# A retimed order of attention, and the combine weights' splits between the experts' relus, in a fused attention and soft-MoE kernel

## The chip, the cores and the metric

The kernel runs as one program on one core of a Trainium2 chip. Its time is what the device takes for one execution, in microseconds. The core's engines are TensorE (PE; its weight loads are shown apart as PEld), VectorE (DVE), ScalarE (ACT), GpSimd (POOL) and SyncE (SP), which here issues nearly all transfers. Each engine works through its own list of instructions in order and waits at an instruction until what it needs is there.

## What is computed

First comes attention with a memory, for 8 batches and 8 heads of 576 positions and 64 columns; its output is laid out as 4608 rows of 512 and goes through a soft mixture of 8 experts with 4 slots each.

```python
scores = np.where(causal, -1e9, scale * q @ k.T)
local  = softmax(scores) @ v
q_p    = where(q > 0, q, exp(q) - 1) + 1
mem    = (q_p @ M_prev) / (q_p . z_prev + 1e-6)
x      = g * mem + (1 - g) * local            # g = sigmoid(beta) per head
logits = x @ phi                              # 4608 x 32
slot_in = softmax(logits, over rows).T @ x    # 32 x 512
slot_out[e] = relu(slot_in[e] @ w1[e]) @ w2[e]
out    = softmax(logits, over slots) @ slot_out
```

All inputs are float32. The expert weights alone are 32 MB (64 tiles of 512 KB).

## The kernel before

**The attention** is done in 32 steps n = 0 to 31, one for each batch and pair of heads (`@n` in the tables). The order in which all its small operations are written is a table, SEQ, with 2546 entries, each the name of an operation, its step and, for the ones that take a PSUM bank, the bank's number behind a colon. A second table, EV, says for each copy and some arithmetic which engine does it (`a` ScalarE, `v` VectorE, `p` GpSimd). A loop calls `op_<name>` entry by entry, and `pin()` then fixes every engine's instructions in just this order. WORD says into which freed tile the last weight tiles are loaded.

The operations that matter below:

- `loadq`, `loadk`, `loadv`, `loadm`: a step's inputs, each one transfer on SP; `w@x`: one weight tile of 512 KB on SP.
- `qhi`, `qlo`, `kn`, `kl` (L359, L403, L409): q and k split into a rounded part and a rest for the score products `s.*` (L414, L433, L441); `max.*` (L470), `exp.*` (L478), transposes `t.*` (L567), their copies `te.*` (L354, L357).
- `qmin`, `qexp`, `qphi` (L510 on ScalarE or L512 on GpSimd, L515, L519): the feature map, in the tile `qp`, of which there is one for even and one for odd steps.
- `norm`, `neps`, `nmk`, `nred` (L525 to L542): the memory's normaliser. `nrw` (L547) writes it to a scratch in DRAM, `rd`; `nrr` (L553) reads it back, spread over the partitions, as `rb`; `qn` (L557) multiplies it into `qp`; `mema` uses that.
- `rec` (L483, L484), `rt`, `rte`: the softmax's reciprocal; `rrw` (L498 to L500) writes it to DRAM as `rs`, `rrr` (L504) reads it back into a part of the tile `rm`; `mo` (L631) and `xe.0` (L638, L639) multiply the local output with it, `xe.1` (L642) adds the memory's. `rb` and this part of `rm` exist once, so each read waits for the last use of the step before.
- `x*` and `y*`: the slots' running softmax and sums, once for every finished block of 512 rows, with the last block in `y*`.

**The tail** is ordinary code behind the table (L1015 to L1051): `f1(eg, f)` multiplies the slots with w1 (16 matmuls in float32, shown as 32 by the profile) and applies the relu on ScalarE (L940); `f1t` transposes the result; `f2(dh, eg, f)` multiplies with w2 and sums over all eg, f into one PSUM bank per output half dh. `c1`, `c2` do the last two blocks' softmax over slots and its transposes; `c3(i, j)` splits the transposed combine weights `cT` into a rounded part, twice, by ScalarE, and a rest, by VectorE (L989), for tile j of `cst4` (i = 0, 32 x 1024) or of `cst8` (i = 1, 32 x 128). `g1`, `g2` scale and split the slots' output; `comb(dh, t4)` makes 512 rows of an output half in two PSUM banks (4 matmuls), which ScalarE and VectorE copy out, one each, and SP stores them (512 KB). 20 weight tiles are loaded during the tail, into the tiles that the first `f1` have read. PSUM there: two banks for `f1` and `f2`, two for `f1t`, `c1`, `c2`, `g2`, four for `comb`.

Of the kernel before, what the change touches and what calls it, by code (L numbers as in the profile page):

```python
# [51 lines left out]
max.q2h0@1 t.3@0:1 rte@0 exp.a@1 qphi@1 t.4@0:0 rrw@0 exp.b@1 s.z@1:0 max.q3h0@1 te.4@0 te.3@0 te.1@0 loadk@3 s.q1@1
exp.q2h0@1 norm@1:3 max.q3h1@1 av.0@0:0 kn@2 max.q1h0@1 exp.q3h0@1 max.z@1 s.b@2:1 qn@0 av.1@0 neps@1 exp.z@1 nmk@1
rrr@0 s.a@2 av.2@0 max.q1h1@1 exp.q1h0@1 qhi@2 nred@1 mema@0:21 exp.q1h1@1 qlo@2 max.a@2 nrw@1 kl@2 exp.q3h1@1 av.6@0
memb@0 loadm@2 av.3@0 qmin@2 exp.q2h1@1 s.zb@2 loadq@3 s.q2@2 loadv@1 rec@1 s.q1@2:0 max.b@2 max.zb@2 t.0@1:3 exp.b@2
xe.0@0 s.z@2 te.0@1 nrr@1 mo@0 rt@1:1 t.5@1:3 xe.1@0 rte@1 qexp@2 t.4@1:0 rrw@1 max.q1h0@2 te.5@1 t.1@1:1 max.q1h1@2
t.3@1:2 max.q2h1@2 te.1@1 t.2@1:3 max.q2h0@2 loadk@4 exp.a@2 x3.0@0:1 te.3@1 max.z@2 te.4@1 s.q3@2:1 qphi@2 exp.q1h0@2
s.zb@3:0 qhi@3 max.q3h0@2 av.0@1:2 te.2@1 loadq@4 kn@3 x3e.0@0 qn@1 rrr@1 s.b@3 exp.q1h1@2 norm@2:0 kl@3 max.q3h1@2
av.3@1 exp.q2h1@2 mema@1:13 qlo@3 exp.q3h1@2 max.zb@3 neps@2 av.6@1 nmk@2 qmin@3 loadm@3 exp.q2h0@2 s.q3@3:1 nred@2
exp.z@2 s.q2@3 max.q3h1@3 nrw@2 exp.q3h0@2 av.1@1 max.q2h0@3 max.q3h0@3 exp.q3h1@3 memb@1 av.2@1 xe.0@1 qexp@3 loadv@2  # L60
s.q1@3:1 rec@2 exp.q2h0@3 qphi@3 t.1@2:0 rt@2:3 nrr@2 s.z@3 max.b@3 rte@2 mo@1 exp.q3h0@3 s.a@3 kn@4 norm@3:3
max.q1h0@3 te.1@2 max.q2h1@3 rrw@2 t.3@2:2 qhi@4 neps@3 t.0@2:0 xe.1@1 te.3@2 kl@4 t.4@2:3 te.0@2 exp.q2h1@3 loadq@5
t.2@2:1 loadk@5 qlo@4 te.4@2 t.5@2:2 nmk@3 t.0@3:0 max.a@3 te.2@2 max.q1h1@3 t.2@3:3 nred@3 exp.a@3 qn@2 x3.1@0:1
te.5@2 nrw@3 x3e.1@0 s.q2@4:0 rrr@2 exp.q1h0@3 av.0@2:2 av.2@2 te.0@3 s.zb@4 s.b@4 te.2@3 max.z@3 av.6@2 s.a@4
mema@2:01 exp.b@3 nrr@3 max.zb@4 exp.z@3 av.1@2 max.q2h1@4 qmin@4 loadm@4 max.q2h0@4 memb@2 exp.q1h1@3 av.3@2 max.b@4
exp.q2h1@4 max.a@4 loadv@3 s.q3@4:1 xe.0@2 loadk@6 rec@3 exp.a@4 s.q1@4:0 mo@2 rt@3:3 s.z@4 rte@3 xe.1@2 qexp@4 rrw@3
t.1@3:1 qn@3 exp.b@4 max.z@4 t.4@3:2 te.1@3 t.3@3:3 max.q1h0@4 te.4@3 qphi@4 t.5@3:0 qhi@5 te.3@3 mema@3:21 max.q3h1@4
qlo@5 te.5@3 max.q1h1@4 kn@5 norm@4:3 qmin@5 s.zb@5:0 exp.q1h0@4 av.0@3:0 neps@4 rrr@3 nmk@4 nred@4 s.a@5 s.b@5 av.3@3
kl@5 nrw@4 qexp@5 memb@3 av.2@3 max.zb@5 loadm@5 exp.z@4 x1.0@0:3 qphi@5 av.1@3 exp.q1h1@4 max.q3h0@4 exp.q2h0@4
av.6@3 s.q2@5 exp.q3h1@4 xe.0@3 s.q3@5:1 nrr@4 exp.q3h0@4 mo@3 t.3@4:1 xe.1@3 t.1@4:0 loadv@4 te.3@4 max.q3h1@5 x1.1@0  # L70
loadq@6 te.1@4 norm@5:2 rec@4 loadk@7 x1l@0 t.4@4:1 neps@5 max.a@5 max.q3h0@5 rt@4:0 t.0@4:3 rte@4 te.4@4 x1m@0
t.5@4:2 rrw@4 s.z@5:1 te.0@4 x1e@0 qn@4 t.2@4:0 max.b@5 exp.q3h1@5 w@1 te.5@4 x2@0:1 te.2@4 s.q1@5 max.q2h1@5
exp.q3h0@5 av.0@4:3 max.q1h1@5 max.q2h0@5 qhi@6 exp.b@5 av.1@4 max.q1h0@5 kn@6 max.z@5 exp.q1h0@5 rrr@4 memb@4:2
s.zb@6:0 qlo@6 exp.q2h0@5 s.a@6 kl@6 mema@4:0 exp.q2h1@5 x2m@0 loadq@7 nmk@5 s.b@6 exp.q1h1@5 qmin@6 max.b@6 s.q3@6:1
exp.a@5 nred@5 exp.z@5 max.a@6 av.6@4 nrw@5 av.2@4 max.q3h0@6 av.3@4 max.q3h1@6 exp.q3h0@6 loadv@5 s.q2@6 mo@4 qexp@6
s.q1@6:1 rec@5 x2a@0 s.z@6 exp.a@6 xe.1@4 t.2@5:3 qhi@7 xe.0@4 nrr@5 t.3@5:1 max.q1h0@6 te.2@5 kn@7 rt@5:0 t.0@5:2
te.3@5 rte@5 qlo@7 max.q2h0@6 t.5@5:3 loadm@6 te.0@5 max.q2h1@6 t.4@5:0 rrw@5 te.5@5 kl@7 t.1@5:1 qphi@6 x2e@0
x3.3@0:2 te.4@5 max.q1h1@6 x3.2@0:3 loadq@8 te.1@5 max.zb@6 max.z@6 loadk@8 s.q3@7:0 exp.q2h1@6 qn@5 s.b@7:1
max.q3h1@7 x4.0@0:0 s.a@7 max.q3h0@7 s.zb@7 x3e.3@0 av.0@5:1 rrr@5 x3e.2@0 exp.q3h1@6 norm@6:2 max.a@7 av.1@5
exp.q2h0@6 max.zb@7 x4a.0@0 w@2 neps@6 exp.b@6 memb@5:3 x2s@0 av.6@5 mema@5:0 exp.z@6 exp.q1h1@6 nmk@6 av.2@5 nred@6  # L80
qmin@7 exp.q1h0@6 av.3@5 exp.q3h1@7 x4.1@0:2 nrw@6 xe.0@5 loadm@7 s.q2@7 rec@6 loadk@9 qexp@7 s.q1@7:0 x4a.1@0 loadv@6
mo@5 t.2@6:3 rt@6:2 s.z@7 xe.1@5 rte@6 rrw@6 te.2@6 t.0@6:1 kn@8 t.3@6:2 max.b@7 te.0@6 qhi@8 t.5@6:0 nrr@6 te.3@6
t.4@6:3 qlo@8 qphi@7 te.5@6 t.1@6:1 te.4@6 max.q1h0@7 x3.0@1:2 kl@8 max.z@7 te.1@6 x5@0:0 av.0@6:3 exp.a@7 max.q2h1@7
rrr@6 max.q1h1@7 av.6@6 norm@7:1 max.q2h0@7 av.3@6 neps@7 s.q3@8:0 exp.q1h0@7 loadq@9 nmk@7 exp.q3h0@7 nred@7 av.2@6
qn@6 x5e@0 nrw@7 s.zb@8:1 exp.z@7 s.a@8 av.1@6 w@3 max.q3h0@8 exp.b@7 mema@6:01 max.q3h1@8 exp.q1h1@7 exp.q2h0@7 mo@6
s.b@8 qmin@8 loadm@8 memb@6 exp.q2h1@7 xe.1@6 s.q1@8:0 loadv@7 s.q2@8 exp.q3h0@8 nrr@7 rec@7 xe.0@6 s.z@8 qexp@8
max.zb@8 max.a@8 max.q2h0@8 t.4@7:3 kn@9 x3e.0@1 qhi@9 rt@7:0 t.1@7:1 te.4@7 kl@9 rte@7 t.3@7:2 max.b@8 rrw@7 te.1@7
max.q2h1@8 x3.1@1:0 max.z@8 t.2@7:3 x3e.1@1 qlo@9 t.0@7:1 max.q1h0@8 loadk@10 t.5@7:0 qphi@8 te.0@7 qn@7 s.q3@9:1
te.3@7 max.q1h1@8 te.5@7 exp.z@8 s.q2@9:0 exp.q2h1@8 norm@8:1 rrr@7 s.zb@9 mema@7:02 neps@8 exp.q3h1@8 max.zb@9 nmk@8
max.q3h1@9 exp.b@8 av.0@7:1 w@4 te.2@7 qmin@9 loadq@10 nred@8 s.b@9 exp.q2h0@8 memb@7 av.1@7 max.q3h0@9 nrw@8 qexp@9  # L90
loadm@9 max.b@9 s.a@9 av.3@7 exp.q1h0@8 qphi@9 av.6@7 av.2@7 exp.a@8 exp.q1h1@8 mo@7 loadv@8 s.q1@9:1 exp.q3h1@9
# [193 lines left out]
def tile_attn_soft_moe(ctx, tc, q, k, v, M, beta, phi, w1, w2, cst, out):  # L285
# [718 lines left out]
    def comb(dh, t4):  # L1004
# [8 lines left out]
        nc.sync.dma_start(out=out[512 * t4:512 * t4 + 512, 256 * dh:256 * dh + 256].rearrange("(u a) d -> a u d", a=128), in_=o)  # L1013
# [104 lines left out]
```

## Time and profile before

| | us |
|---|---|
| median of 3 runs | 483.08 (481.46 to 484.53) |
| the profiled execution | 482.45 |
| its span, first to last instruction | 480.7 |
| PE busy | 431.5 (90%) |
| DVE busy | 378.3 (79%) |
| ACT busy | 341.2 (71%) |
| POOL busy | 168.8 (35%) |

Times in the profile count from the first instruction of the span. A row of busy groups gives the line, engine and operation, `out<-in` with shapes, the count, then busy us, mean ns of one, and the idle time just ahead of them with what ended it. A row of waits reads: engine, line, `<-` what ended the wait, then us in total, times, longest. A piece of the chain that ended last is: start, length, engine or DMA, and what. The chain follows back, from the end, what released each step. DMA share is the mean busy share of the core's 16 DMA engines. PE busy counts the modelled length of each matmul.

### The profile page before, as it was taken

Reading aid. Unit: us, or ns where it says so; the run is one execution under the profiler, and the core shown is the slowest. Engines: PE = TensorE matmul, PEld = TensorE weight load, DVE = VectorE, ACT = ScalarE, POOL = GpSimd, SP = SyncE. Lnnn points to the kernel's source line nnn. Section 1 sums busy time; section 2 is a strip of 40 time slices with the busy share of each in tenths; the row PEclk is TensorE's granted clock in tenths of the full one; section 3 lists DMA queues with packets and bytes.
Section 4 is the critical chain, followed back from the end, with each engine's and each line's share of the span. In section 5 each row is a group of like instructions: output and inputs, shape, how many; then the busy total and the mean of one; then the engine's idle time right before and its main releaser. Section 6 shows DMA issues by size and latency. Waiting matters only on the chain.

```text
span 480.7 us, 15438 instructions
## 1 busy us (share of the span) xinstructions
PE 431.5 (90%) x5762; PEld 288.1 (60%) x5762; DVE 378.3 (79%) x1289; ACT 341.2 (71%) x1001; POOL 168.8 (35%) x155
## 2 busy tenths in 40 slices
...
GB/s 259 152 204 163 114 243 192 216 195 146 157 190 238 209 222 166 203 155 181 192 218 199 179 234 243 202 261 169 222 202 145 157 275 285 244 412 410 154 342 312
DMA packets 65658, 104.09 MB, mean 217 GB/s; under 512 B 10608, under 2 KB 40880, under 8 KB 65584
## 3 DMA queue, kind: packets, MB, share of 16 engines
...
q10 hardware_dynamic: 288, 0.09, 0.1%
...
## 4 chain that ended last, share of the span: by engine, by line
PE 32%; DMA 27%; DVE 21%; ACT 5%; POOL 5%; issue 4%; SPq 4%; DVEq 0%; POOLq 0%; ACTq 0%
DMA rb<-rd 10%; DMA rm<-rs 9%; PE psT L414 9%; DVE q L470 4%; PE psS L441 4%; PE psT L567 4%; PE pf L937 3%; DVE zq L470 3%; DMA rd<-rq 3%; DVE qp L519 2%; DVE at L357 2%; PE pc L1011 2%; ACT w L354 2%; POOL qp L557 2%; PE pf L954 2%
## 5 line engine op out<-in xcount | busy, mean ns | idle before, releaser
L414 PE MATMUL psT<-at,mv 128*32 128x64 f32 (+4 forms) x1536 | 103.4, 389 | 2.3 <-DMA mv<-in_v_dram 2.1
L354 ACT COPY at<-psT 128x256 f32<-128x256 f32 (+1 forms) x209 | 87.3, 481 | 23.9 <-PE psT L567 21.4
L478 ACT ACTIVATE q<-q,nm 128x384 f32<-128x384 f32 (+2 forms) x160 | 97.7, 614 | 8.4 <-DVE nm L470 5.7
L470 DVE CUSTOM_DVE_ANT_0 q<-psS,mv 128x512 f32<-128x512 f32 (+1 forms) x128 | 76.6, 612 | 5.0 <-PE psS L441 2.6
L441 PE MATMUL psS<-K,X 64*128 64x512 f32 (+2 forms) x576 | 72.3, 364 | 5.0 <-DVE nm L470 2.6
L567 PE MATMUL psT<-cs,q 128*128 128x128 f32 x480 | 70.0, 275 | 1.2 <-ACT q L478 0.6
L478 ACT ACTIVATE zq<-zq,nm 128x256 f32<-128x256 f32 (+2 forms) x128 | 68.0, 536 | 3.0 <-DVE nm L470 2.9
L441 PEld LDWEIGHTS psS<-K,X 64*128 64x128 f32 x576 | 45.2, 184 | 27.5 <-issue 9.5
L414 PEld LDWEIGHTS psT<-at,mv 128*32 128x32 f32 x1536 | 40.4, 110 | 32.6 <-issue 20.6
L567 PEld LDWEIGHTS psT<-cs,q 128*128 128x128 f32 x480 | 55.6, 141 | 4.0 <-issue 1.0
L557 POOL TENSOR_TENSOR qp<-qp,rb 128x576 f32<-128x576 f32 x23 | 33.5, 1458 | 53.1 <-DMA rb<-rd 39.0
L567 PE MATMUL psT<-cs,zq 128*128 128x128 f32 x288 | 46.8, 279 | 3.7 <-DVE xt L631 3.3
L512 POOL TENSOR_SCALAR qp<-qq 128x576 f32<-128x576 f32 x19 | 31.8, 1672 | 42.6 <-PE psT L414 41.2
L414 PE MATMUL psT<-qp,q 128*32 128x64 f32 (+1 forms) x512 | 37.3, 408 | 5.0 <-POOL qp L557 2.7
L567 PEld LDWEIGHTS psT<-cs,zq 128*128 128x128 f32 x288 | 34.1, 143 | 6.0 <-DVE xt L631 3.7
L409 POOL TENSOR_TENSOR K<-k,K 128x512 fp32r<-128x512 f32 x25 | 35.6, 1424 | 1.3 <-DVE K L357 0.4
L631 DVE TENSOR_TENSOR xt<-psT,rm 128x448 f32<-128x448 f32 (+7 forms) x60 | 23.6, 432 | 12.9 <-DMA rm<-rs 8.8
L414 PEld LDWEIGHTS psT<-qp,q 128*32 128x32 f32 x512 | 15.0, 109 | 31.0 <-issue 19.5
L357 DVE COPY at<-psT 128x512 f32<-128x512 f32 (+1 forms) x52 | 29.4, 585 | 4.6 <-PE psT L567 1.9
L359 POOL TENSOR_SCALAR K<-k 128x512 fp32r<-128x512 f32 x22 | 14.9, 675 | 50.6 <-PE psS L433 29.2
L519 DVE SCALAR_TENSOR_TENSOR qp<-qq,qp 128x576 f32<-128x576 f32 x32 | 31.1, 973 | 0.3 <-ACT qp L515 0.2
L478 ACT ACTIVATION_READ_ACCUMULATOR q<-q,nm 128x1 f32 x160 | 31.3, 196 | 0.0
...
## 6 DMA issues: line engine op xcount, KB each, us to landing
...
```

What stands on the lines that cost most here:

```text
L354: nc.scalar.copy(o, i)
L357: nc.vector.tensor_copy(out=o, in_=i)
L409: ALU_ENG[ev("kl", n)].tensor_tensor(out=K2[:, 1, :], in0=st[n]["k"][:, 0:512], in1=K2[:, 0, :].bitcast(F32), op=ALU.subtract)
L414: nc.tensor.matmul(o[32 * g:32 * g + 32], w[:, 32 * g:32 * g + 32], x(g), start=start, stop=stop)
L441: nc.tensor.matmul(ps[:, c0:c0 + N], X[ROW[h], x, 128 * i - 128:128 * i], K2[ROW[h], y, 0:N], start=(x, y) == (0, 0), stop=(x, y) == (0, 1))
L470: nc.vector.tensor_tensor_reduce(out=sm, in0=src, in1=msk, op0=ALU.add, op1=ALU.min, scale=-0.125, scalar=m0, accum_out=acc_o)
L478: nc.scalar.activation(sm, sm, AF.Exp, scale=-1.0, bias=s["nm"][:, J:J + 1], accum_out=s["sum"][:, J:J + 1])
L512: ALU_ENG[ev("qmin", n)].tensor_scalar(out=st[n]["qp"], in0=st[n]["q"], scalar1=0.0, scalar2=None, op0=ALU.min)
L519: ALU_ENG[ev("qphi", n)].scalar_tensor_tensor(out=t, in0=st[n]["q"], scalar=0.0, in1=t, op0=ALU.max, op1=ALU.add)
L557: ALU_ENG[ev("qn", n)].tensor_tensor(out=s["qp"], in0=s["qp"], in1=s["rb"], op=ALU.mult)
L567: nc.tensor.transpose(out=ps[:, 128 * x:128 * x + 128], in_=src[:, k0:k0 + 128], identity=ident)
L631: nc.vector.tensor_tensor(out=o, in0=st[n]["oa"][:, c0:c1], in1=rr[:, 64 + c0:64 + c1], op=ALU.mult)
```

## The change

SEQ has the same 2546 operations in another order, with other PSUM banks; EV gives some of them to another engine; WORD has other numbers. The tables' first lines show their kind:

```diff
-gate@0 loadq@1 loadm@0 loadk@1 w@0 qmin@0 qhi@0 qlo@0 qexp@0 kn@0 s.zb@0:0 s.a@0 s.b@0 kl@0 qmin@1 qphi@0 loadk@2
+gate@0 loadm@0 loadq@1 w@0 loadk@1 loadm@1 loadv@0 qmin@0 qhi@0 qlo@0 qexp@0 kn@0 s.a@0:0 s.zb@0 s.b@0 kl@0 qphi@0
```

In EV, `qmin` goes from 13 on ScalarE and 19 on GpSimd to 22 and 10; `qlo` from 14 on VectorE and 18 on GpSimd to 7 and 25; `kn` from 7 on ScalarE, 3 on VectorE and 22 on GpSimd to 2, 2 and 28; `kl` from 7 on VectorE to 6, `qhi` from 5 to 4, `nmk` from 16 to 19, `neps` from 21 to 20 (the rest on GpSimd, for `neps` on ScalarE); the copies `te` stay at 152 and then 151 on ScalarE of 192. 

In the table the distances between a transfer's issue and what uses it change. Mean number of entries over the 32 steps, before and now: `nrw` to `nrr` 23.5 and 31.2, `nrr` to `qn` 32.2 and 36.3, so `nred` to `qn` 60.8 and 74.4; `rrw` to `rrr` 26.9 and 33.1, `rrr` to the first of `mo` and `xe.0` 29.7 and 30.5 (the smallest 15 and 21), so `rec` to that first use 74.6 and 80.5.

What this does on an engine, VectorE in step 19, from the reciprocal of its normaliser on, before:

```order
L542 RECIPROCAL rq<-rq 128x9
L483 SCALAR_TENSOR_TENSOR r<-sum,rm 128x9
L484 RECIPROCAL r<-r 128x9
L638 TENSOR_TENSOR xt_3327<-psT_4124,rm 128x64
L639 TENSOR_TENSOR xt_3327<-xt_3327,psT_4124 128x64
L631 TENSOR_TENSOR xt_3327<-psT_4083,rm 128x192
L631 TENSOR_TENSOR xt_4154<-psT_4083,rm 128x320
L470 ISA q_4174,nm<-psS_4068,mv 128x384
L470 ISA nm 128x1
L642 TENSOR_TENSOR xt_3327<-xt_3327,psT_4129 128x192
```

and now:

```order
L543 RECIPROCAL rq<-rq 128x9
L471 ISA q_4079,nm<-psS_4056,mv 128x512
L471 ISA nm 128x1
L358 COPY at<-psT_4033 128x2x256
L471 ISA q_4112,nm<-psS_4068,mv 128x384
L471 ISA nm 128x1
L471 ISA q_4112,nm<-psS_4068,mv 128x384
L471 ISA nm 128x1
L708 TENSOR_REDUCE s_4141<-rm 128x4
L709 TENSOR_SCALAR s_4141<-s_4141 128x4
L710 RECIPROCAL s_4141<-s_4141 128x4
L711 TENSOR_TENSOR rm<-rm,s_4141 128x128
```

Before, the previous step's row `rm` is used three rows behind the reciprocal; now the first use (`xt<-psT,rm`) stands sixteen rows behind it, and the multiply with `rb` that follows, L557 (now L558), 44 rows behind it where it was 35.

SP in steps 30 and 31 (`rd`, `rb`: normaliser; `rs`, `rm`: softmax row; `in_w`: weights; L389 loads v), before:

```order
L500 DMA rs<-rts 2x1x64
L754 DMA qq<-in_w_dram 128x1024
L754 DMA K_6511<-in_w_dram 128x1024
L754 DMA q_6520<-in_w_dram 128x1024
L504 DMA rm<-rs 64x576 x2
L547 DMA rd<-rq 128x9
L757 DMA zq<-in_w_dram 128x1024
L757 DMA X<-in_w_dram 128x1024
L498 DMA rs<-rts 2x3x128
L499 DMA rs<-rts 2x2x64
L500 DMA rs<-rts 2x1x64
L389 DMA mv<-in_v_dram 128x768
```

and now:

```order
L755 DMA K_6482<-in_w_dram 128x1024
L554 DMA rb<-rd 64x4x144 x2
L505 DMA rm<-rs 64x576 x2
L548 DMA rd<-rq 128x9
L755 DMA X<-in_w_dram 128x1024
L755 DMA qq<-in_w_dram 128x1024
L499 DMA rs<-rts 2x3x128
L500 DMA rs<-rts 2x2x64
L501 DMA rs<-rts 2x1x64
L390 DMA mv<-in_v_dram 128x768
L554 DMA rb<-rd 64x4x144 x2
L758 DMA zq<-in_w_dram 128x1024
```

The two halves of the read of step 30's row (`rm<-rs ... x2`) stand behind three weight loads before, and behind one weight load and the read of `rb` of the same step now; the loads of X and qq follow it.

The tail is written in another order:

```diff
             (act, dve)[half](o[:, 2 * half:2 * half + 2, :], ps)
         nc.sync.dma_start(out=out[512 * t4:512 * t4 + 512, 256 * dh:256 * dh + 256].rearrange("(u a) d -> a u d", a=128), in_=o)
 
+    c1(7)
+    c1(8)
     f1(0, 0)
+    c2(7)
+    c2(8)
     f1(0, 1)
     f1t(0, 0)
-    c1(7)
-    c1(8)
+    c3(0, 0)
+    c3(0, 1)
     f1(1, 0)
     f1t(0, 1)
-    c2(7)
-    c2(8)
+    c3(0, 2)
+    c3(0, 3)
     f1(1, 1)
     f1t(1, 0)
-    c3(0, 0)
     f2(0, 0, 0)
     f1t(1, 1)
     for x, (pool, name) in enumerate(reload):
         wload(nw + x, pool, name)
-    for j in range(1, 4):
-        c3(0, j)
     for j in range(4):
         c3(1, j)
     f2(0, 0, 1)
     f2(0, 1, 0)
     f2(0, 1, 1)
     g1(0)
-    f2(1, 0, 0, (0,))
+    f2(1, 0, 0, (0, 1))
     g2(0)
-    f2(1, 0, 0, (1, 2, 3))
+
+    parts = [(0, 0, (2, 3)), (0, 1, (0, 1)), (0, 1, (2, 3)), (1, 0, (0, 1)), (1, 0, (2, 3)), (1, 1, (0, 1)), (1, 1, (2, 3))]
     for t4 in range(NQ):
         comb(0, t4)
-        if t4 == 4:
-            f2(1, 0, 1)
-    f2(1, 1, 0)
-    f2(1, 1, 1)
-    g1(1)
-    g2(1)
+        if t4 < 7:
+            f2(1, *parts[t4])
+        if t4 == 6:
+            g1(1)
+        if t4 == 7:
+            g2(1)
     for t4 in range(NQ):
         comb(1, t4)
     pin()
```

ScalarE in the tail (`qp<-pf`: the relus; `CAST w<-cT`, `CAST xk<-cT`: `c3`; `CAST k<-pp`: `g2`; `lt`, `ex`: `c1`; `cT<-pp`: `c2`), before:

```order
L940 ACTIVATE qp<-pf 128x512 x2
L966 ACTIVATE lt<-lt 128x128
L966 ACTIVATE ex<-ex 128x128
L940 ACTIVATE qp<-pf 128x512
L354 COPY cT<-pp 128x128 x2
L940 ACTIVATE qp<-pf 128x512
L354 CAST w_7054<-cT 32x1024 x2
L354 CAST w_7121<-cT 32x1024 x2
L354 CAST w_7125<-cT 32x1024 x2
L354 CAST w_7129<-cT 32x1024 x2
L354 CAST xk<-cT 32x128 x8
L354 CAST k<-pp 96x256
```

and now:

```order
L967 ACTIVATE lt<-lt 128x128
L967 ACTIVATE ex<-ex 128x128
L941 ACTIVATE qp<-pf 128x512
L355 COPY cT<-pp 128x128 x2
L941 ACTIVATE qp<-pf 128x512
L355 CAST w_7004<-cT 32x1024 x2
L355 CAST w_7008<-cT 32x1024 x2
L941 ACTIVATE qp<-pf 128x512
L355 CAST w_7037<-cT 32x1024 x2
L355 CAST w_7041<-cT 32x1024 x2
L941 ACTIVATE qp<-pf 128x512
L355 CAST xk<-cT 32x128 x8
L355 CAST k<-pp 96x256
```

The wide splits stood behind the last relu and now stand between the last three. On VectorE their subtractions stand, likewise, two by two ahead of the copies of `f1t`, and `g1` comes behind the four short ones of `cst8`. `f2(1, ...)` is cut into pieces of 8 matmuls, one before `g2(0)` and one behind each of the first seven combines of the first half; `g1(1)` and `g2(1)` come behind the seventh and the eighth combine.

More of the change, by code (lines that the diff above doesn't have):

```diff
@@ L52 @@
[L52 to L91, printed above, removed]
@@ new lines @@
+rrr@3 norm@4:3 te.4@3 exp.b@4 qhi@5 mema@3:02 exp.q3h1@4 neps@4 qlo@5 nmk@4 s.b@5:1 exp.q2h1@4 nred@4 av.0@3:1 loadm@5
+kn@5 qmin@5 max.z@4 nrw@4 av.2@3 kl@5 qexp@5 max.b@5 w@2 av.3@3 exp.q1h1@4 loadq@6 av.1@3 qphi@5 exp.q3h0@4 av.6@3
+x1.0@0:3 exp.z@4 mo@3 memb@3 s.q2@5 loadv@4 xe.1@3 s.q3@5:0 loadk@6 xe.0@3 norm@5:1 rec@4 s.zb@5 s.a@5 nrr@4
+max.q3h1@5 x1.1@0 neps@5 t.3@4:0 x1l@0 max.q3h0@5 nmk@5 rt@4:2 t.0@4:1 x1m@0 rte@4 t.5@4:3 te.3@4 rrw@4 max.q2h0@5
+t.4@4:2 exp.b@5 s.z@5:0 max.q2h1@5 te.0@4 max.zb@5 te.5@4 te.4@4 t.2@4:0 w@3 x1e@0 loadq@7 s.q1@5 max.a@5 te.2@4
```

396 lines of the change are left out of this document (216 added, 180 removed).

## The prediction

> **What bounds the kernel now.** I read the page first (busy shares, the chain that ended last), then the engines by stage (busy time per stretch), then what VectorE waited for in each part of the program, and then the end of the chain and the timeline at the two places where it stands still. The page:
>
> ```profile
> PE 431.5 (90%) x5762; PEld 288.1 (60%) x5762; DVE 378.3 (79%) x1289; ACT 341.2 (71%) x1001; POOL 168.8 (35%) x155
> PE 32%; DMA 27%; DVE 21%; ACT 5%; POOL 5%; issue 4%; SPq 4%; DVEq 0%; POOLq 0%; ACTq 0%
> ```
>
> TensorE is busy for 90% of the span, yet a quarter of the chain is transfers: no engine is simply full. The stretches (PE busy, PEld, DVE, ACT, POOL, clock, DMA share, GB/s):
>
> ```profile
> 0.00:380.00 380.00, 353.95 (x4892) 241.20 (x4892) 331.74 (x1176) 299.55 (x908) 166.35 (x153) 1.00 0.66 195
> ...
> 416.00:442.00 26.00, 24.96 (x284) 10.63 (x284) 9.37 (x20) 11.32 (x16) 0.00 (x0) 1.00 0.90 354
> 442.00:446.00 4.00, 0.33 (x5) 0.24 (x2) 2.83 (x6) 2.73 (x9) 0.00 (x0) 1.00 0.80 320
> 446.00:451.00 5.00, 5.00 (x37) 2.73 (x36) 1.23 (x3) 1.43 (x3) 0.00 (x0) 0.66 0.03 11
> 451.00:479.00 28.00, 16.65 (x161) 11.50 (x160) 11.89 (x19) 9.54 (x18) 0.00 (x0) 0.84 0.99 338
> ```
>
> So there are three regimes. Up to 380 us TensorE (93%) and VectorE (87%) take turns at being late. From 416 to 442 the experts run back to back under weight loads. From 451 on the stores fill the DMA engines (share 0.99, 338 GB/s): the end stands at a fixed distance from the first store. Between these lie two holes, 380 to 405 and 442 to 451; in the second the DMA engines, too, idle (0.03).
>
> **The change part by part.** Its three places are the middle of the attention, its last two pairs, and the tail.
>
> *The middle, 0 to 380.* What VectorE waited for there, of transfers:
>
> ```profile
> DVE qp L557 <- DMA rb<-rd: 4.1, 3, 2.0
> DVE xt L638 <- DMA rm<-rs: 3.4, 5, 1.1
> DVE xt L631 <- DMA rm<-rs: 3.3, 4, 1.5
> ```
>
> 10.8 us in 12 waits, 1.4 us each for `rb` and 0.74 us each (6.7/9) for `rm`. The work of the 32 pairs is 2546 entries of SEQ in about 405 us, 0.16 us an entry. In the table the way from `nred` over both transfers of the normaliser to `qn` grows from 60.8 entries on average to 74.4, by 2.2 us; from `rec` to the first use of its row (`mo` or `xe.0`) from 74.6 to 80.5, by 0.9 us. Both exceed the mean wait at their end, so by this most of the 10.8 us goes. I count half of it, because TensorE at 93% has 26 us of idle in this stretch from other causes too, and what VectorE no longer waits for will partly be waited for elsewhere: -5. The ends are -18 (all of it, and the 7 us of work that leaves VectorE, below) and +8 (the rival on ScalarE).
>
> The engines of the small steps change as well. The rows that price them:
>
> ```profile
> L512 POOL TENSOR_SCALAR qp<-qq 128x576 f32<-128x576 f32 x19 | 31.8, 1672 | 42.6 <-PE psT L414 41.2 <-DVE nm L470 1.4
> L510 ACT ACTIVATE qp<-qq 128x576 f32<-128x576 f32 x13 | 8.9, 683 | 11.9 <-POOL rn L537 5.0 <-issue 3.9 <-DMA qq<-in_q_dram 2.6
> L403 DVE TENSOR_TENSOR X<-qq,X 128x576 fp32r<-128x576 f32 x14 | 14.7, 1052 | 0.2
> L354 ACT CAST K<-k 128x512 fp32r<-128x512 f32 x7 | 4.4, 628 | 2.0 <-issue 1.0 <-PE psS L433 1.0
> ```
>
> Nine more `qmin` go from GpSimd to ScalarE: 9 x 0.68 = +6.1 us there and 9 x 1.67 = -15.0 on GpSimd. Seven more `qlo` go from VectorE to GpSimd: 7 x 1.05 = -7.4 on VectorE. Five `kn` leave ScalarE, 5 x 0.63 = -3.1, for GpSimd. The other moves (`kl`, `qhi`, `nmk`, copies of banks) are of one to three instructions each and about cancel. I cost all of these at nothing: GpSimd is busy 166 of 380 us and ScalarE 300 of 380, which covers its net +3, and VectorE's relief of 7 us only counts where VectorE is what is late; if ScalarE's cover is gone, the +3 shows.
>
> *The last two pairs.* Here the transfer is visibly the chain:
>
> ```profile
> 386.86 7.66 DMA rm<-rs
> ...
> 397.47 6.04 DMA rm<-rs
> ```
>
> In front of the first of these reads three weight loads stand on the same queue (the rows of SP above, in the section on the change). Its issue, and VectorE's waits in this stretch:
>
> ```profile
> 386.30 1.15 SPq L504 DMA_DIRECT2D rm<-rs  x2
> ```
>
> ```profile
> DVE xt L631 <- DMA rm<-rs: 5.4, 1, 5.4
> DVE qp L557 <- DMA rb<-rd: 2.0, 1, 2.0
> DVE xt L638 <- DMA rm<-rs: 1.9, 1, 1.9
> ```
>
> A load of 512 KB (0.524 MB) at the 354 GB/s of 416 to 442 takes 1.48 us. In the new order one such load stands ahead of this read in place of three, and 2 x 1.48 = 3.0 us go; the reads of `rb` of the same pair now come just before it, which I let take as long to issue (1.15 us), partly beside the rest. I take -2.5. The ends: -7.3 if both waits for `rm` go (5.4 + 1.9), +2 if `rb` and the later weights delay the last pair's read by as much as its own longest wait for `rm` or `rb` (1.9, 2.0). The two weight loads that are moved behind it cost nothing as long as they land before the experts read them, some 30 us later; if they don't, each costs its 1.48 us.
>
> *The tail.* The chain and the timeline at the second hole:
>
> ```profile
> 424.78 3.69 PE pf L937 x32
> ...
> 429.74 3.61 PE pf L937 x32
> 433.43 0.60 ACT qp L940
> 434.03 0.92 ACT w L354
> ...
> 441.33 1.05 ACT w L354
> 445.22 0.50 DVE k L996
> ```
>
> ```profile
> 416.01 7.07 PE L937 MATMUL pf<-w,at 128*32 128x512 f32 x64 [0.67 <-DVE dt L885]
> ...
> 424.32 0.28 DVE L963 TENSOR_REDUCE m<-pp 128x4 f32<-128x128 f32 x1
> ...
> 427.96 0.29 DVE L971 TENSOR_TENSOR ex<-ex,s 128x128 f32<-128x128 f32 x1
> ...
> 441.69 0.40 PE L954 MATMUL pf<-w,at 128*32 128x256 f32 x4
> 442.40 1.22 DVE L989 TENSOR_TENSOR w<-cT,w 32x1024 fp32r<-32x1024 f32 x1 [0.91 <-ACT w L354]
> ...
> 445.76 0.70 PE L1000 MATMUL pp<-k,cs 128*128 128x256 f32 x2 [3.67 <-DVE k L996]
> 446.39 2.79 PE L954 MATMUL pf<-w,at 128*32 128x256 f32 x24
> 446.89 0.42 DVE L1002 TENSOR_TENSOR k<-pp,k 32x256 fp32r<-32x256 f32 x1 [1.19 <-ACT k L354]
> 449.11 3.76 PE L1011 MATMUL pc<-k,w 96*128 96x256 f32 x20
> 450.95 4.77 SPq L1013 DMA_DIRECT2D out_dram<-w  x5
> 452.80 1.93 PE L954 MATMUL pf<-w,at 128*32 128x256 f32 x32
> 454.66 1.57 PE L1011 MATMUL pc<-k,w 96*128 96x256 f32 x9
> ```
>
> The experts' products of the first half end at 442.09, but the scaling `g1` (L996) stands on VectorE behind the splits of the combine weights (`c3`), which ScalarE only begins after its last relu: 3.1 us until 445.22. TensorE idles 3.67 us, its granted clock falls to 0.66 in the next stretch, and 24 products take 2.79 us; at the pace of 452.80 (32 in 1.93) they would take 1.45. In the new order the eight wide copies of `c3` lie between the relus. They took 442.38 - 434.03 = 8.35 us. Half of them, 4.2 us, and a relu (0.60) come on each interval between the last three `f1`, which is now 429.74 - 424.78 = 4.96 us and gets shorter by the two transposes: ScalarE just holds this, and the last relu slips by at most some 1.3 us, which `f2(0,0,0)` (32 as at 452.80, 1.9 us) covers. VectorE's part, 1.22 us each, now stands ahead of the copies of `f1t`, two by two; that delays them by up to 2.4 us, and `f2` asks for each of these copies only after another group of 32 products (1.93 us) and a transpose, so I cost it at nothing, at 0.5 us if it doesn't fit. The new chain: 442.1, `g1` 0.5 beside 16 products (16/32 x 1.93 = 0.97), so 443.1; `g2` 0.70; its copy and subtraction 0.85 (446.46 to 447.31 now): 444.7 for the first combine instead of 449.11, -4.4. The two transposes of `c1` leave the place between `f1(0,1)` and `f1(1,0)`, where they and their wait took up to 1.7 us (416.01 + 7.07 = 423.08 to 424.78, with four transposes of `f1t` in it), for one ahead of `f1(0,0)`, where TensorE waits 0.67 us anyway; but `c2(8)` may now wait some 0.5 us for VectorE's two chains of softmax (428.25 - 424.32 = 3.9 us, from about 416.1, against an end of `f1(0,0)` at 419.5): -0.3 net. Against that, every combine is now followed by 16 products: 4/9 x 1.57 + 0.97 = 1.67 us each, while a store takes 0.524 MB / 338 GB/s = 1.55 us. Over seven of them, with `g2(1)` in between, the stores starve by about 1.0 us. Sum: -3.7. The ends: -2 (3.1 saved, the clock still low, 1 us of starving) and -5 (no starving). The floor under this are the weight loads, which fill the DMA engines until about 445 in either order; a first store at 446.5 is behind them.
>
> **The sum.** The profiled run took 482.45 us, its span of 480.7 and 1.75 around it, 0.6 below the median of 483.08, within the three runs' spread. 482.45 - 5 - 2.5 - 3.7 = 471.25, say 471.5.
>
> The page "DMA: Bandwidth & Descriptors" of the Trainium skill, section "Anatomy of one DMA", speaks against the first two terms: it fits a copy issued from GpSimd with 2.0 us plus its bytes at 436 GB/s, an estimate of 2.3 us for one of 144 KB, and by that neither chain would ever be waited for, and the sum would be 478.75. This case's trace differs:
>
> ```profile
> 262.82 3.10 DMA rb<-rd
> ...
> 344.97 6.64 DMA rb<-rd
> ```
>
> The same small read takes 3.1 us one time and 6.6 another, so the slack of an average is not enough for each, and slack in the order is worth something; the first rival keeps the other possibility.
>
> **The rivals.**
>
> *Only the tail gains.* (The time that the page's rule gives, too.) The waits of the middle are taken over by others (VectorE idles for GpSimd's `rn`, for TensorE's banks), and the last pair's read waits for its own weights. For it: the three transfer waits are 10.8 of 380 us, and TensorE is at 93%. Against it: the waits are where the chain runs. 482.45 - 3.7 = 478.75.
>
> *All transfer waits go.* 10.8 us, of the last pairs' waits the longest, 5.4, and the tail: 482.45 - 10.8 - 5.4 - 3.7 = 462.6. For it: every distance in the table grew. Against it: some waits of an engine always reappear on another.
>
> *ScalarE becomes late (slower).* Its place is `qmin` in ScalarE's queue: it may only overwrite `qp` once `mema` of the pair before last has read it (L414). On GpSimd this waited 41.2 us in 14 times, at no cost. On ScalarE `qmin` waited 11.9 us in 13, 0.9 us each, and behind it queue the exponentials on which the transposes hang. Nine more: 9 x 0.9 = 8.2 us, with the net 3 us of work. It decides if ScalarE's waits at L510 come to over 15 us and TensorE's idle follows. With no gain before 416: 482.45 + 8 - 3.7 = 487. Against it: in the table `qmin` on ScalarE stands 9.9 entries behind that `mema` on average, before 8.5.
>
> *The end does not move.* The stores starve behind the interleaved products as long as the hole was, and the rest is neutral: 482.
>
> **How the numbers follow.** Chances: the forecast (467 to 476) 0.45; only the tail 0.24; all waits 0.13; the end does not move 0.09; ScalarE 0.09. About 1% (4.8 us) is what a measurement of this kernel tells from no change, so faster means under 478.3. Faster: 0.45 + 0.13 and half of the tail case, 0.12, together 0.70; same: the other half, 0.12, and 0.09, together 0.21; slower 0.09. The range: below, it takes in most of the case without waits, 462; above, the tail case and its scatter, 481; left out are ScalarE's case, most of the unmoved end and some below.
>
> **What would show it.** Right: the DVE waits for `rm` and `rb` fall from 20 us to under 10; the chain no longer holds a read of `rm` of over 7 us; PE's wait before the first L1000 is under 1 us, the clock there stays at 1.0 and the first store is issued about 31 us after `f1` begins (now 450.95 - 416.01 = 34.9). Wrong: ACT's idle before L510 above 15 us; DVE idle shifted to banks or to `rn`; or a DMA share well under 0.99 while the stores run.

## The result, and the profile after

| | before | changed |
|---|---|---|
| time, median of 4 runs | 483.32 us (481.46 to 484.53) | 468.61 us (465.73 to 469.78) |
| ratio | | 0.9697, 95% interval 0.9651 to 0.9743 |
| profiled execution, its own time and span | 482.45, 480.7 us | 465.73, 463.9 us |

The change makes the kernel 14.7 us faster; the forecast was 471.5, in a range of 462 to 481. The profiled execution of the changed kernel is the fastest of its four (the others took 468.3 to 469.8), so its stages add up to some 2 us more of gain (16.8 us by the spans) than the medians; where the two differ, the medians decide. Ratios leave out executions that stand more than 1.5% above the fastest of their kernel; of one kernel below, the changed one with the old engines, two of ten took 830 us, and the profiled one is among these. Lines of the changed kernel's code stand one further down than before (`L510` is now `L511`).

The page of the changed kernel, busy shares and the chain that ended last:

```profile
PE 429.7 (93%) x5762; PEld 284.9 (61%) x5762; DVE 376.8 (81%) x1287; ACT 342.0 (74%) x1000; POOL 169.9 (37%) x158
PE 47%; DMA 17%; DVE 17%; issue 5%; POOL 5%; SPq 3%; ACT 2%; DVEq 0%; POOLq 0%; ACTq 0%
```

The engines' work is nearly the same (TensorE 431.5 us before, VectorE 378.3); what is gone is waiting, and from the chain it is the transfers that left, 27% before and 17% now. Within them the reads of `rb` went from 10% of the span to 3%, those of the row from 9% to 10%. The stretches of the changed kernel (PE busy, PEld, DVE, ACT, POOL, clock, DMA share, GB/s):

```profile
0.00:380.00 380.00, 362.14 (x4980) 247.15 (x4981) 336.55 (x1197) 308.99 (x933) 168.83 (x157) 1.00 0.69 199
380.00:404.00 24.00, 21.90 (x307) 14.15 (x305) 14.29 (x43) 8.07 (x23) 1.06 (x1) 1.00 1.00 337
404.00:407.50 3.50, 2.88 (x30) 1.12 (x32) 2.49 (x10) 0.62 (x2) 0.00 (x0) 1.00 0.36 142
407.50:433.00 25.50, 24.55 (x288) 10.50 (x282) 11.05 (x19) 14.26 (x25) 0.00 (x0) 1.00 0.99 394
433.00:462.00 29.00, 18.17 (x174) 12.00 (x166) 12.42 (x20) 10.10 (x18) 0.00 (x0) 0.87 0.99 343
```

In the first 380 us TensorE is busy for 362.1 us, 353.95 before. The second hole, with its DMA share of 0.03 and its clock of 0.66, is gone: from 407.5 us to the end the DMA engines are at 0.99, first with the weight loads, then with the stores. The experts' first half in the same order of rows as shown of before (the timeline of the changed kernel):

```profile
404.78 3.64 PE L938 MATMUL pf<-w,at 128*32 128x512 f32 x32 [0.61 <-DVE at L876]
...
429.32 0.48 DVE L997 TENSOR_SCALAR k<-pf,dt 128x256 f32<-128x256 f32 x1 [3.06 <-PE pf L955]
430.05 0.70 PE L1001 MATMUL pp<-k,cs 128*128 128x256 f32 x2
...
431.66 0.74 PE L1012 MATMUL pc<-k,w 96*128 96x256 f32 x4 [0.92 <-DVE k L1003]
...
433.19 0.40 SPq L1014 DMA_DIRECT2D out_dram<-w  x1
```

`g1` (L997) now waits 3.06 us for TensorE, where TensorE had waited 3.67 us for it; the first store is issued 433.19 - 404.78 = 28.4 us after the experts begin, 34.9 before.

VectorE's waits for the two small transfers over the whole program, changed kernel:

```profile
DVE xt L639 <- DMA rm<-rs: 6.9, 4, 2.7
DVE xt L632 <- DMA rm<-rs: 4.5, 5, 2.0
DVE qp L558 <- DMA rb<-rd: 2.9, 3, 1.3
```

and of the kernel before:

```profile
DVE xt L631 <- DMA rm<-rs: 8.8, 5, 5.4
DVE qp L557 <- DMA rb<-rd: 6.2, 4, 2.0
DVE xt L638 <- DMA rm<-rs: 5.3, 6, 1.9
```

20.3 us have become 14.3: less, but more than half is still there. Other traces of the same two tables give 18.3 us for the old one and 13.5 and 17.5 for the new. This list is VectorE's alone, and `qn` runs on GpSimd for 23 of the 32 steps, where it waits longer, before and now:

```profile
POOL qp L557 <- DMA rb<-rd: 39.0, 13, 5.8
```

```profile
POOL qp L558 <- DMA rb<-rd: 27.4, 11, 7.0
```

VectorE's list shows another change: the waits in the normaliser's own arithmetic, for TensorE and GpSimd, went from 9.8 us to 1.5, a larger drop than that of its waits for transfers. Before:

```profile
DVE rq L541 <- POOL rn L537: 6.0, 6, 2.7
DVE rn L532 <- PE psT L525: 3.8, 6, 1.4
```

and now:

```profile
DVE rq L542 <- POOL rn L538: 0.8, 2, 0.4
DVE rn L533 <- PE psT L526: 0.7, 2, 0.5
```

SP's queue stands still until a write has landed before it issues the read. These waits of SP, before:

```profile
SPq L504 <- DMA rs<-rts: 23.9, 21, 3.0
SPq L553 <- DMA rd<-rq: 21.8, 14, 3.1
```

and now:

```profile
SPq L505 <- DMA rs<-rts: 9.6, 11, 2.1
SPq L554 <- DMA rd<-rq: 6.4, 7, 2.7
```

45.7 us have become 16.0. What these waits were worth is for the experiments to say.

### The profile page after: what moved, and what is told of

The parts are those of the page before. It is cut to its first block, busy times and chain, and to the rows that moved or that the text cites. A ratio compares the mean times of both kernels' runs of the same rounds, so it can differ in the third digit from the quotient of the medians.

```text
span 463.9 us, 15411 instructions
## 1 busy us (share of the span) xinstructions
PE 429.7 (93%) x5762; PEld 284.9 (61%) x5762; DVE 376.8 (81%) x1287; ACT 342.0 (74%) x1000; POOL 169.9 (37%) x158
## 4 chain that ended last, share of the span: by engine, by line
PE 47%; DMA 17%; DVE 17%; issue 5%; POOL 5%; SPq 3%; ACT 2%; DVEq 0%; POOLq 0%; ACTq 0%
PE psT L415 15%; DMA rm<-rs 10%; PE psS L442 8%; PE psT L568 5%; DMA rb<-rd 3%; PE pf L955 3%; PE pf L938 3%; DVE zq L471 3%; PE psS L434 3%; DVE q L471 2%; PE pc L1012 2%; DMA rs<-rts 2%; DVE qp L520 2%; PE psS L415 2%; DVE xt L632 1%
## 5 line engine op out<-in xcount | busy, mean ns | idle before, releaser
L355 ACT COPY at<-psT 128x512 f32<-128x512 f32 (+1 forms) x208 | 86.8, 488 | 29.4 <-PE psT L568 22.9
L479 ACT ACTIVATE q<-q,nm 128x512 f32<-128x512 f32 (+2 forms) x160 | 98.0, 617 | 3.9 <-PE psT L415 1.7
L415 PE MATMUL psT<-at,mv 128*32 128x64 f32 (+4 forms) x1536 | 99.8, 389 | 0.8 <-DMA mv<-in_v_dram 0.4
L442 PE MATMUL psS<-K,X 64*128 64x512 f32 (+2 forms) x576 | 70.7, 362 | 3.4 <-DVE nm L471 1.9
L479 ACT ACTIVATE zq<-zq,nm 128x576 f32<-128x576 f32 (+2 forms) x128 | 68.4, 538 | 5.2 <-DVE nm L471 5.1
L558 POOL TENSOR_TENSOR qp<-qp,rb 128x576 f32<-128x576 f32 x23 | 34.3, 1491 | 34.3 <-DMA rb<-rd 27.4
L568 PE MATMUL psT<-cs,zq 128*128 128x128 f32 x288 | 45.2, 274 | 0.6 <-DVE xt L640 0.6
L360 POOL TENSOR_SCALAR K<-k 128x512 fp32r<-128x512 f32 x28 | 19.3, 688 | 70.0 <-PE psS L434 43.5
L360 POOL TENSOR_SCALAR X<-qq 128x576 fp32r<-128x576 f32 x28 | 19.3, 691 | 60.6 <-PE psS L434 36.0
L415 PE MATMUL psT<-qp,q 128*32 128x64 f32 (+1 forms) x512 | 37.2, 407 | 3.2 <-DVE qp L558 2.2
L404 POOL TENSOR_TENSOR X<-qq,X 128x576 fp32r<-128x576 f32 x25 | 37.8, 1513 | 1.4 <-DVE X L358 0.4
L415 PEld LDWEIGHTS psT<-qp,q 128*32 128x32 f32 x512 | 15.3, 109 | 27.8 <-issue 22.6
L434 PE MATMUL psS<-K,X 128*128 128x256 f32 x192 | 31.0, 296 | 1.0 <-DVE K L410 0.6
```

The source lines that it names most:

```text
L355: nc.scalar.copy(o, i)
L360: ENG = dict(a=act, v=dve, p=lambda o, i: nc.gpsimd.tensor_scalar(out=o, in0=i, scalar1=1.0, scalar2=1.0, op0=ALU.mult, op1=ALU.mult))
L404: ALU_ENG[ev("qlo", n)].tensor_tensor(out=X[:, 1], in0=st[n]["qx"], in1=X[:, 0].bitcast(F32), op=ALU.subtract)
L415: nc.tensor.matmul(o[32 * g:32 * g + 32], w[:, 32 * g:32 * g + 32], x(g), start=start, stop=stop)
L434: nc.tensor.matmul(o, X[:, x, 448:576], K2[:, y, x0:x1], start=(x, y) == (0, 0), stop=(x, y) == (0, 1))
L442: nc.tensor.matmul(ps[:, c0:c0 + N], X[ROW[h], x, 128 * i - 128:128 * i], K2[ROW[h], y, 0:N], start=(x, y) == (0, 0), stop=(x, y) == (0, 1))
```

## The experiments

Times are medians; each group of four kernels shared its chip with the kernel before (484.56, 484.59 and 483.13 us). Ratios are to it, and microseconds are worked out from them at 483.3.

**The two halves of the change.** The changed tables (SEQ, EV, WORD) with the whole tail as it was, a diff to the changed kernel:

```diff
-    c1(7)
-    c1(8)
     f1(0, 0)
-    c2(7)
-    c2(8)
     f1(0, 1)
     f1t(0, 0)
-    c3(0, 0)
-    c3(0, 1)
+    c1(7)
+    c1(8)
     f1(1, 0)
...
```

> The new SEQ, EV and WORD with the tail of the kernel before. If the two halves of the change act apart (my theory, from the two traces: f1 starts 11 us earlier, the tail behind it is 5.6 us shorter), this is 9 to 11 us faster than the kernel before, 472 to 474 us, ratio 0.978 to 0.981. Rival, the tail only gains because the order brings the weights to it earlier: then this alone gives 14 us, 469.

And the whole changed tail with the tables as they were, a diff to the kernel before:

```diff
+    c1(7)
+    c1(8)
     f1(0, 0)
+    c2(7)
+    c2(8)
     f1(0, 1)
     f1t(0, 0)
-    c1(7)
-    c1(8)
+    c3(0, 0)
+    c3(0, 1)
     f1(1, 0)
...
```

> The order of the kernel before with the new tail. My theory: 4 to 6 us faster than before, 477.5 to 479.5 us, the wait ahead of the first combine gone and its clock at 1.0. Rival (the two halves need each other): 0 to 2 us.

Tables alone: 474.5 us, ratio 0.9813 (0.9765 to 0.9861), -9.0. Tail alone: 476.47 us, 0.9846 (0.9791 to 0.9901), -7.4. Multiplied they give 0.966; the whole change measured 0.9697. Both halves gain, and about alike; the tail gains more than the 4 to 6 us expected.

**The waits taken out.** Before and changed, with the multiplications that wait for `rb` (`qn`) and for the row (`mo`, `xe.0`) reading a column of ones; all transfers stay, and nothing waits for them. The normaliser and the sums of the softmax are left out of the result.

```diff
-        ALU_ENG[ev("qn", n)].tensor_tensor(out=s["qp"], in0=s["qp"], in1=s["rb"], op=ALU.mult)
+        ALU_ENG[ev("qn", n)].tensor_tensor(out=s["qp"], in0=s["qp"], in1=uno.broadcast_to([128, S]), op=ALU.mult)
...
```

The two lines of `mo` and `xe.0` change likewise, with the column in the place of `rr`.

> The kernel before, in which the multiplies with the two rows read back from DRAM take a column of ones in their place: all transfers stay, but nobody waits for these two (the normaliser and the softmax's sum are left out of the result). If the middle of the attention gained by slack for these transfers, this gains at least as much, 9 to 14 us, 469 to 474. If it gained by something else (other engines, order of the arithmetic), this gains at most 5 us: 478 or more.

> The same done to the changed kernel (the same two rows left out). If the slack is what the new order brought, little is left to gain here: 0 to 4 us below the changed kernel, 465 to 469. If the transfers' waits cost both kernels alike, it gains as much as the kernel before does by the same edit.

Before: 472.2 us, 0.9734 (0.9658 to 0.9809), -12.9. Changed: 463.02 us, 0.9576 (0.9533 to 0.962), -20.5, so 5.9 below the changed kernel. That is more than the 0 to 4 expected of it. Without the waits the two kernels differ by 7.6 us, which is what the tail alone gains (7.4): by the times the two bodies are then equal, within a scatter of some 4 us. So these waits were worth about 13 us in the old order and 6 in the new, and the difference, 7, is as large as the body's gain (0.9697 against 0.9846, 7.2 us; 9.0 by the tables alone). The profiled executions leave a rest: with the waits in, the experts begin at 416.01 and 404.78 us, without them at 404.02 and 400.12, so 3.9 of 11.2 us are still there. By these figures the room for the transfers is from two thirds of the body's gain to all of it. What the rest is, if there is one, stays open: VectorE's waits in the normaliser's arithmetic are a candidate (5.4 us in the kernel before without the waits, 1.7 in the changed one), and no run takes these away. The constant also makes `qn` on GpSimd shorter, 1393 ns against 1458 in the old order and 1258 against 1491 in the new, and how much of the gains is due to that was not measured.

SP's standing still, on the other hand, has no price of its own that these runs resolve. In the kernel before without the waits it is nearly all there, and in the changed kernel without them 15.6 us are left:

```profile
SPq L506 <- DMA rs<-rts: 23.6, 22, 2.6
SPq L555 <- DMA rd<-rq: 18.6, 17, 2.4
```

**Which of the two waits.** The normaliser alone out of the way (only the `qn` line of the diff above; left out of the result is the normaliser), before and changed:

> The kernel before, with the normaliser alone out of the way: qn multiplies by a column of ones, the transfers of the normaliser stay, nothing waits for them. Left out of the result: the normaliser. Both multiplications freed gave -12.9 us. Theory that the room for the normaliser is the larger part (VectorE's waits for it fell from 4.1 to 1.3 us between the two kernels, those for the row rose from 6.7 to 8.4): -8 us or more, 476. Rival, the row's read carries it: -4 or less, 480.

> The changed kernel with the normaliser alone out of the way, as in the run beside it. If the changed order has made the room for the normaliser already, nothing is left here: -1.5 us or less, 467 to 469.5, and what the full freeing gave (-5.6) is the row's. Rival: half of it or more, -3 us, 465.5.

Before: 480.71 us, 0.9956 (0.9923 to 0.999), -2.1. Changed: 468.46 us, 0.9683 (0.9633 to 0.9734), the changed kernel itself. My theory that the room for the normaliser is the larger part fell. The trace of before without the normaliser shows why:

```profile
DVE xt L633 <- DMA rm<-rs: 13.4, 7, 3.4
DVE xt L640 <- DMA rm<-rs: 8.9, 7, 5.5
```

VectorE's waits for the row rose from 14.1 to 22.3 us: 6.2 us of waits for `rb` went, 8.2 came for the read that follows it. GpSimd's 39.0 us of waits for `rb`, and the 10% of the chain that these reads had, went with the 6.2, and all of this was worth 2.1 us. Freeing the waits for the row too brings another 10.7 us before (0.9956 to 0.9734) and 5.2 in the changed kernel, so the time lies with the row once `rb` is out of the way; the row alone was not freed, and whether `rb` would then hold up the rest isn't shown.

**The engines against the order.** The changed kernel with the whole EV of before (its first row here, with the sign of the diff), and the kernel before with the whole changed EV, the same with the signs turned:

```diff
 EV = {o: e for e, x in dict(
     a="""
-        qmin@0 qmin@1 neps@0 te.4@0 te.1@0 rte@0 te.3@0 te.5@0 te.0@1 qmin@2 te.5@1 te.4@1 te.2@1 x3e.0@0 neps@2 te.1@1 qmin@3
+        qmin@0 qmin@1 neps@0 te.2@0 te.0@0 te.5@0 rte@0 te.4@0 te.3@0 kn@2 te.0@1 rte@1 te.5@1 te.1@1 te.3@1 te.4@1 te.2@1
...
```

> The changed order, list of weights and tail, with the engines of the small steps as before. With the waits taken out, the experts began at 404.0 us in the kernel before and at 400.1 in the changed one, with them in at 416.0 and 404.8: by that some 7 of the 11 us by which they begin earlier come from the room that the order gives the transfers, and 4 are open. Theory of the room: undoing the engines costs 4 us at most, 469 to 473. Rival, the engines (nine qmin off GpSimd, seven qlo off VectorE) carry the gain: 476 or more. An order planned for other engines may fit these badly; the next run looks at the same from the other side.

> The kernel before with the new engines of the small steps alone: order, list of weights and tail stay. Prediction: costed at nothing, so 482 to 485, the kernel before within 1%. Theory of the room: at most the 4 us that are open, 480. Rival, the engines carry the gain: 476 or less. Rival on ScalarE (its nine qmin late): 490.

The theory of the room fails in both runs; the rival, that the engines carry the gain, has its 476 or more in the first and misses its 476 or less in the second by 20 us. The changed kernel with old engines: 484.28 us, 1.0006 (0.9958 to 1.0054), all of the gain gone, the tail's too (no trace of it is used). The kernel before with new engines: 496.08 us, 1.026 (1.0168 to 1.0352), 12.6 us slower. In the latter's trace the waits for transfers have become small, 2.8 and 2.5 us for the row and 1.6 for `rb`, and others stand in their place (TensorE's and ScalarE's, kernel before with new engines):

```profile
PE psS L441 <- DVE nm L470: 7.8, 9, 2.1
PE psS L414 <- DVE nm L470: 4.1, 7, 0.9
```

```profile
L510 ACT ACTIVATE qp<-qq 128x576 f32<-128x576 f32 x22 | 15.0, 684 | 18.0 <-issue 9.8 <-PE psT L414 5.4 <-DMA qq<-in_q_dram 1.9
```

TensorE waits 7.8 + 4.1 us for VectorE's `nm`, 2.6 + 2.8 in the kernel before. And ScalarE's idle time ahead of `qmin` (L510) is 18.0 us, 5.4 of it for `mema` and 9.8 for nothing that the profile shows: in its total the picture that the rival on ScalarE had drawn. Whether `qmin` causes the loss, the next pair tells.

**`qmin` alone.** Its fifteen changed engines on the kernel before, and its old ones in the changed kernel:

```diff
+EV.update({o: e for e, x in dict(
+    a="qmin@2 qmin@3 qmin@5 qmin@8 qmin@11 qmin@12 qmin@14 qmin@18 qmin@20 qmin@24 qmin@25 qmin@29",
+    p="qmin@16 qmin@19 qmin@26",
+).items() for o in x.split()})
```

> The kernel before with the new engines of qmin alone: twelve go from GpSimd to ScalarE and three the other way, nothing else. All new engines on the old order cost +12.6 us, where the prediction costed them at nothing. Rival on ScalarE (qmin in its queue waits for mema and holds up the exponentials): +8 us, 492, with ScalarE's idle time ahead of L510 over 15 us. Otherwise it is the steps on GpSimd and VectorE: within 3 us of the kernel before.

> The changed kernel with the old engines of qmin alone. All old engines on the new order cost 15 us. If qmin is what ties the order to the engines, 478 or more; if it is the many small steps together, 470 to 474; prediction (engines at nothing): 468.6 within 2.

On the kernel before: 486.16 us, 1.0048 (1.0001 to 1.0095), +2.3. In the changed kernel, taken back: 468.53 us, 0.9693 (0.9653 to 0.9734), no difference. So `qmin` alone does not tie the order to the engines; the rival on ScalarE has its sign and a quarter of its price, and the idle time ahead of `qmin` is 14.8 us in that trace, not over 15. What loses the other 10 us in the crossed kernels is among the moves of `qlo`, `kn`, `kl`, `nmk`, the copies and the rest, and is left open.

**The loads ahead of the last but one row.** The changed kernel with `w@30` and `w@31` back ahead of `rrr@30`:

```diff
-... w@29 te.4@30 ... rrr@30 ... w@30 x4a.0@6 ... w@31 ...
+... w@29 w@30 w@31 te.4@30 ... rrr@30 ... x4a.0@6 ...
```

> The changed kernel with the two weight loads w@30 and w@31 put back ahead of the row's read of the pair before the last, so that three loads stand there again. Prediction's step: +2.5 to +3.0 us, 471.4. Rival: the read is hidden by then or the chain goes by other work, within 1 us of the changed kernel, 468 to 469.5.

471.25 us, 0.9772 (0.9703 to 0.9842): 3.6 us slower than the changed kernel by the ratios, 2.6 by the medians, but the two intervals overlap, so its size is not settled. The trace shows where the loads went in (SP in this kernel, and then VectorE's wait from 376 us to the experts' start):

```profile
376.96 0.34 SPq L755 DMA_DIRECT2D K<-in_w_dram  x1
377.35 0.42 SPq L755 DMA_DIRECT2D X<-in_w_dram  x1
378.16 0.33 SPq L755 DMA_DIRECT2D qq<-in_w_dram  x1
378.53 1.85 SPq L554 DMA_DIRECT2D rb<-rd  x2
380.49 1.27 SPq L505 DMA_DIRECT2D rm<-rs  x2
```

```profile
DVE qp L558 <- DMA rb<-rd: 5.2, 1, 5.2
```

Behind three loads it is now the read of `rb` that comes 5.2 us late.

**The splits put back.** The changed kernel with `c3` behind the last relu and the reload again, the combines still interleaved:

```diff
     f1t(0, 0)
-    c3(0, 0)
-    c3(0, 1)
     f1(1, 0)
     f1t(0, 1)
-    c3(0, 2)
-    c3(0, 3)
     f1(1, 1)
     f1t(1, 0)
+    c3(0, 0)
     f2(0, 0, 0)
...
+    for j in range(1, 4):
+        c3(0, j)
     for j in range(4):
         c3(1, j)
```

> The changed kernel with the splits of the combine weights back behind the last relu and the reload; the combines stay interleaved with the products, and c1 and c2 stay early. Prediction's step: the wait for the scaling and the lower clock behind it come back, +4.4 us, 473. Rival, that the end is set by the bytes (weights of the second half and stores, which now run without a gap): +1.5 or less, 470.

474.38 us, 0.9842 (0.9771 to 0.9913): 5.8 us above the changed kernel by the medians, 7.0 by the ratios. The wait is back (timeline and stretch of this kernel):

```profile
432.51 2.77 PE L955 MATMUL pf<-w,at 128*32 128x256 f32 x48
...
436.49 1.47 DVE L990 TENSOR_TENSOR xk<-cT,xk 32x128 fp32r<-32x128 f32 x4
437.99 0.48 DVE L997 TENSOR_SCALAR k<-pf,dt 128x256 f32<-128x256 f32 x1
438.53 1.07 PE L1001 MATMUL pp<-k,cs 128*128 128x256 f32 x2 [3.24 <-DVE k L997]
...
442.53 5.46 SPq L1014 DMA_DIRECT2D out_dram<-w  x3
```

```profile
440.00:445.00 5.00, 4.49 (x28) 2.66 (x32) 1.31 (x3) 1.18 (x3) 0.00 (x0) 0.50 0.32 111
445.00:474.00 29.00, 17.25 (x162) 11.36 (x154) 12.09 (x19) 9.50 (x17) 0.00 (x0) 0.85 0.90 309
```

`g1` (L997) stands behind the splits on VectorE again (L990), 2.7 us after the products are done at 435.28. TensorE idles 3.24 us, its clock falls to 0.50, and the first store comes 442.53 - 409.96 = 32.6 us after the experts begin, 4.2 later than in the changed kernel, close to the prediction's 4.4. And the products between the combines run at that clock, so the stores starve (share 0.32, then 0.90) and the rest takes another 1.7 us (474.9 - 442.53 = 32.4, against 463.9 - 433.19 = 30.7).

## Why the prediction was right, and where it was not

**The sum** came out: 471.25 forecast, 468.61 measured. By halves, the attention was forecast at -5 - 2.5 = -7.5 and measured -9.0 (tables alone); the tail was forecast at -3.7 and measured -7.4, 4.8 at the least. By the two profiles the tail gained 5.6 us (64.7 us from the experts' start to the end before, 59.1 now). So the tail was sized too small and the attention about right; that the attention's term came out is in part luck, since its evidence was not what I had made of it and a term that I had put at nothing, the engines, is not small.

**The middle, "most of the 10.8 us goes".** The step that failed is the one from the distances to the waits. Up to 380 us, VectorE's waits for `rb` fell from 4.1 to 1.3 us as forecast, but those for the row rose from 6.7 to 8.4, and over the whole program the sum fell from 20.3 to 14.3, not under 10. The mechanism holds in the sum: without these waits both bodies take the same time within some 4 us, and the changed order leaves 6 us of them where the old had 13. But it was not readable from the list of VectorE's waits, which leaves out GpSimd's 39.0 us for `rb` (27.4 now). What a wait is worth and how long it is are two things: VectorE's 6.2 us and GpSimd's 39.0 us of waits for `rb` were together worth 2.1 us, since the row's read came late next, while 45.7 us of SP's waits had no price that can be seen.

**"The same small read takes 3.1 us one time and 6.6 another."** I set this against the page "DMA: Bandwidth & Descriptors" of the Trainium skill, section "Anatomy of one DMA", by whose fit neither chain would ever be waited for and the time would be 478.75. The runs decide for the trace: with the waits taken out the kernel before gains 12.9 us, and in the changed kernel, too, the last two reads of the row take 5.61 and 5.94 us (its chain of waits; 7.66 and 6.04 before):

```profile
377.47 5.61 DMA rm<-rs
...
386.60 5.94 DMA rm<-rs
```

**"I cost all of these at nothing", the engines.** In the change as a whole this did no harm, but it was wrong as a statement on the engines: they are worth 12.6 us on the old order, against, and some 15 us on the new one, for. ScalarE's and GpSimd's free time did not cover them. My working looked at how much work an engine has (VectorE's relief of 7 us, ScalarE's net 3). That it is instead the order, which row stands ahead of which on an engine, fits both runs and isn't shown, as the moves that cost the most were not found.

**The last two pairs, -2.5.** From the issue of step 30's read to the start of the experts it was 29.7 us before and 27.8 now, -1.9. Other traces of the same rows scatter from 28.7 to 30.7 (old order) and from 27.5 to 30.7 (new), so one trace doesn't resolve this term, and putting the loads back (+2.6 to +3.6, intervals overlapping) doesn't either. It has the forecast's sign and size, and isn't shown.

**The tail, -3.7.** The wait and the clock, -4.4: right. From the end of the first half's products to the first combine it was 7.0 us (442.09 to 449.11) and is 2.4 (429.3, where `g1` starts, to 431.66), -4.6; with the splits put back 4.2 of it return. `c1` and `c2`, "-0.3 net": too small. The last `f1` began 429.74 - 416.01 = 13.7 us after the first one; now it is 417.33 - 404.78 = 12.6 (changed kernel, chain of waits):

```profile
417.33 3.57 PE pf L938 x32
```

That is -1.2: I had let the new `c2(8)` wait 0.5 us for the softmax, and it waits for nothing that counts; the other 0.4 us lie in the rest of that estimate. Up to the end of the first half's products it is 26.1 us before and 24.5 now, -1.6, and from the first combine to its store another -0.3. With the -4.6 this brings the first store not to about 31 but to 28.4 us behind the start (28.4 to 29.9 in five other kernels with this tail, 34.9 to 37.2 in six with the old one; the longer times are those of traces in which the clock fell as the experts began, see the end). The floor that I set under it, weight loads until about 445, moved along: the loads end as the stores begin, and the DMA engines no longer rest in between.

Of the signs that I had named, TensorE's wait ahead of L1001 is gone, the chain holds no read of the row above 5.94 us, and the first store came early; VectorE's waits are the one that failed.

**Starving stores, +1.0:** right. From the first store to the end it takes 30.7 us, 29.75 before, and the share shows it (changed kernel):

```profile
435.00:436.00 1.00, 1.00 (x16) 0.77 (x16) 0.21 (x1) 0.45 (x1) 0.00 (x0) 1.00 0.89 299
...
438.00:450.00 12.00, 11.36 (x105) 7.78 (x97) 7.82 (x14) 6.59 (x12) 0.00 (x0) 1.00 0.94 320
```

**The rivals.** Only the tail gains (478.75): out, the tables alone gain 6.7 us at the least. All waits go (462.6): out, they go in the kernel without them, which takes 463.02, where the changed kernel takes 468.61. ScalarE late (487): in the changed kernel its idle time ahead of L511 is 13.8 us, under the 15 I had named, and `qmin` alone costs 2.3 us on the old order. I had also read its price wrong: none of the waits named in the row of L510 (11.9 us in 13) is for `mema`; they are 5.0 us for GpSimd's `rn`, 3.9 of issue and 2.6 for the transfer of q. The 18.0 us came with the new engines on the old order, along with a loss of 12.6 us that `qmin` alone doesn't make. The end does not move: out.
